# Turning attention probabilities with one stream transpose per head and moving the blocks by SBUF-to-SBUF transfers

## The chip, the cores and the metric

One core of a Trainium2 chip. The metric is the device time of one launch in microseconds (us), as a median of several runs. Each profile shows one execution on the chip.

## What is computed

Chunked attention with a few memory keys, then a two-layer network on its output:

```python
for c in range(S // 32):                       # S = 768, 4 batches, 8 heads of 64
    k_full = concat([mem_k, k[:, :, l_start:r_end]])   # 8 memory rows, 16 left, 32 own, 8 right
    scores = q_c @ k_full.T / 8;  a = softmax(scores)
    out_c = a @ v_full
x = out as (3072 tokens, 512)
h = x @ w_in                                   # 512 x 2048
g = s * relu(h) ** 2 + b
return g @ w_out                               # 2048 x 512
```

The weights arrive in 64 bits and are turned to floats on the chip. Every operand of a large product is split into a high and a low part (gH and gL, x high and x low, H and L of a weight), and a product is three matmuls.

## The kernel before

Tokens are worked on in eight pieces `ch` of 384 (two for each batch). For the first two batches (`ch` 0 to 3) the network runs directly: 64 steps `u`, each `hidden(u)` (line 811, 12 matmuls of 384 columns, L819) and `result(u)` (line 834, 9 matmuls of 512 columns, L843), with relu, square and affine on ScalarE (L827 to L830) and the low part gL on VectorE (L831) in between. For the last two batches the weights are combined (`mix`, line 908, L915 to L935), stored to a scratch in DRAM, fetched again (`fetch`, L945), and 16 units (`unit`, L978; `second`, L1028 and L1054) use fewer products.

`weight` (line 767) prepares one half weight: a transfer to one of three `words` tiles (L776), then VectorE (L800, L801, L803, L806) and ScalarE (L790, L796). `words` tiles are shared: weights use them, and a mix takes one for its sums (`m`) and one for each of its two stages.

`attend(ch, d)` (line 621) handles four heads of one piece, 16 visits in all. A visit has 96 matmuls for the scores (L656), two softmaxes `n` = 0, 1 over tiles of 128 x 6 x 64 (`softmax`, L563 to L582; the division is on GpSimd, L582), and later 48 matmuls with the values (L670). The probabilities must be turned before: `ch` 0 and 1 by TensorE (`turn`, line 592), the twelve visits of `ch` 2 to 7 by `flip` (line 609), 16 stream transposes of 32 x 96 (L613) for each softmax, each of which reads three 32 x 32 blocks and writes them to their place in the block-diagonal tile `aT`. What lies off the diagonal was set to zero once (L519).

The order of all work on each engine and of the transfers on SyncE's queue is fixed ahead of the run by a planner (`Plan.lay`, line 227): every operation has a priority (`prio`, mostly the step `u` at which it is due) and an expected duration (`HOLD`), and among those that are ready the lowest priority goes first. In the kernel each engine then works through its list in that order and waits where an operand is late. The planner expects a transfer to have landed 3400 ns (`FAR`) after its bytes were sent, and counts 440 ns on SyncE for an issue. GpSimd and VectorE operations marked `lock` are never planned at the same time. Constants such as `MIX`, `FLIPS`, `PROD`, `CHAIN`, `SECONDS` and `VISITS` are priorities. The score tiles of visit k and the values of visit k - 1 are issued one behind the other on TensorE.

Of the kernel before, what the change touches and what calls it, by code (L numbers as in the profile page):

```python
# [25 lines left out]
P = 128  # L26
QB = 128
# [56 lines left out]
AHEAD = 0.88  # L84
FLIPS = [5.12, 6.59, 6.68, 6.21, 6.01, 5.03, 6.84, 2.85, 10.89, 4.12, 6.97, 6.28]
PROD = [-1.21, 1.4, 1.6, 1.68, 2.1, 3.33, 3.43]
CHAIN = {'11': 2.04, '22': 0.52, '12': 3.22, '21': 4.37}
SECONDS = [2.94, 3.55, 8.0, 3.91]
XSUM = [-0.96, -0.62, 1.09, -0.07]
XSPLIT = [-6.05, -2.28, -0.26, -2.49, 0.78, 0.92, -0.32]  # L90
RBANKS = 2
# [15 lines left out]


PARTS = [0, 4, 10, NF]
# [6 lines left out]
UNIT = 3.75  # L116
VISITS = [41.16, 48.0, 50.14, 54.14, 58.95, 69.41, 72.68, 81.06, 85.03]
TURNED = set()

# [6 lines left out]
for _u, (_, _f) in enumerate(STEPS):  # L126
# [6 lines left out]
            relu=390, square=390, affine=565, high=388, xhigh=388, xhigh0=480, xhigh1=300, wscale=560, whigh=525, copy=270, exp6=480, exp3=340, keep=390, keepv=470, store=480,  # L133
            low=540, rec=90, edge=20, max6=490, max3=280, sub6=500, sub3=300, sum6=560, sum3=310, flip=270, xlow=470, xlow0=640, xlow1=400, wlow=350, wjoin=620, wsign=610, wdiff=610, out=600,
            small=235, part=290, wide=1040, tiny=200, norm6=1000, norm3=650, mul6=470, mul3=270, issue=440,
# [240 lines left out]
def body(ctx: ExitStack, tc: tile.TileContext, qkv, w1, w2, out):  # L376
# [67 lines left out]
    raws = ring("raw", 2, [P, QK], F32)  # L444
    ts_ = ring("t", 4, [QB, 2 * GB, CELL], F32)
    vs_ = ring("v", 2, [P, VW], F32)
    wide_ = [const.tile([P, 2 * GB * QB], F32, name=f"aT{i}") for i in range(2)]
    diags = Ring([x.rearrange("k (m c q) -> k m c q", m=GB, c=NQC) for x in wide_])
    stats = Ring(stat_tiles)
# [67 lines left out]
    op("POOL", "copy", -100, lambda: make_identity(nc, ident), (), (c_id[0],))  # L517
    for i, x in enumerate(wide_):
        op("POOL", "wrest", -99, lambda x=x: nc.gpsimd.memset(x, 0.0), (), (c_diag[i],))  # L519
    c_early, c_w = [fixed() for _ in range(NEARLY)], {x[1:]: fixed() for x in ORDER}  # L520
# [30 lines left out]

    def softmax(a, late, ch, S, t, st, rows, s_rows, fresh, unit=None):

# [3 lines left out]
        sv = lambda: S.tile[:, :2 * GB * CELL].rearrange("q (m k) -> q m k", k=CELL)[:, s_rows, :]  # L557
        tv = lambda: t.tile[:, rows, :]
        top, den, rden = (lambda k=k: st.tile[k][:, rows] for k in range(3))
        wide = lambda x: x().unsqueeze(2).to_broadcast([QB, n8, CELL])  # L560
        key = (rows.start, rows.stop)
        lo, hi, c, b = (0, LEFT, 0, 0) if ch % HALVES == 0 else (LEFT + CHUNK, LEFT + CHUNK + RIGHT, NQC - 1, GB - 1)
        op("DVE", "edge", a + 0.1, lambda: nc.vector.memset(sv()[c * CHUNK:(c + 1) * CHUNK, b::GB, lo:hi], NEG), (), fresh)  # L563
        op("DVE", "max" + size, a + 0.1, lambda: nc.vector.tensor_reduce(top(), sv(), axis=AX.X, op=ALU.max), fresh, (st["m", key],))
        if unit in SPLIT:
            small(a + 0.1, unit, lambda e: e.tensor_scalar(top(), top(), -SCALE, None, ALU.mult), (st["m", key],))
            for m in range(n8):
                op("ACT", "part", late + 0.2, lambda m=m: nc.scalar.activation(tv()[:, m, :], sv()[:, m, :], AF.Exp, bias=top()[:, m:m + 1], scale=SCALE,  # L568
                                                                               accum_out=den()[:, m:m + 1]),
                   (*fresh, st["m", key]), (t[key, m], st["d", key, m]))  # L570
            made_, sums = [t[key, m] for m in range(n8)], [st["d", key, m] for m in range(n8)]
        else:
            op("DVE", "sub" + size, a + 0.1, lambda: nc.vector.tensor_tensor(tv(), sv(), wide(top), ALU.subtract), (*fresh, st["m", key]), (t[key],))  # L573
            op("ACT", "exp" + size, late + 0.2, lambda: nc.scalar.activation(tv(), tv(), AF.Exp, scale=SCALE), (), (t[key],))
            op("DVE", "sum" + size, late + 0.25, lambda: nc.vector.tensor_reduce(den(), tv(), axis=AX.X, op=ALU.add), (t[key],), (st["d", key],))
            made_, sums = [t[key]], [st["d", key]]
# [15 lines left out]
    def turn(a, t, aT, need, unit):  # L592

        tp = Val(ps, "t")
        keep = lambda: tp.tile[:, :TOK].rearrange("k (m q) -> k m q", m=GB)
        tm = lambda m: t.tile.rearrange("q (m r) l -> q m (r l)", r=2)[:, m, :]
        for m in range(GB):
            op("PE", "turn", a + 0.3, lambda m=m: nc.tensor.transpose(keep()[:, m, :], tm(m), ident), (*need(m), c_id[0]), (tp[m],))
        for r in range(2):
            rows = slice(r * CELL, (r + 1) * CELL)  # L600
            to = lambda rows=rows, r=r: aT.tile[rows, :, :, r * CHUNK:(r + 1) * CHUNK]
            fro = lambda rows=rows: keep()[rows].rearrange("k m (c q) -> k m c q", c=NQC)
            got = [tp[m] for m in range(GB)]
            if (*unit, r) in KEEPV:
                op("DVE", "keepv", a + 0.3, lambda to=to, fro=fro: nc.vector.tensor_copy(to(), fro()), [*got, c_diag[0], c_diag[1]], (aT[r],))
            else:
                op("ACT", "keep", a + 0.3, lambda to=to, fro=fro: nc.scalar.activation(to(), fro(), AF.Copy), [*got, c_diag[0], c_diag[1]], (aT[r],))

    def flip(a, t, aT):

        def block(c, r, g):
            rows = slice(r * CELL + g * CHUNK, r * CELL + (g + 1) * CHUNK)
            nc.vector.transpose(aT.tile[rows, :, c, r * CHUNK:(r + 1) * CHUNK],  # L613
                                t.tile[c * CHUNK:(c + 1) * CHUNK, r::2, g * CHUNK:(g + 1) * CHUNK])

        for c in range(NQC):
            for r in range(2):
                for g in range(CELL // CHUNK):
                    op("DVE", "flip", a + 0.3, lambda c=c, r=r, g=g: block(c, r, g), [*t.parts.values(), c_diag[0], c_diag[1]], (aT[c, r, g],))

    def attend(ch, d):
# [41 lines left out]
        aT = []  # L663

        def value(m, V):
            for c in range(NQC):
                for n in range(2):
                    half, at = divmod(((m * NQC + c) * 2 + n) * D, VW)
                    to = V[m // 2].tile.rearrange("k (m r c q) -> k m r c q", r=2, c=NQC, q=CHUNK)[n * D:(n + 1) * D, m % 2, :, c, :]
                    nc.tensor.matmul(to, vals_[half].tile[:, at:at + D], aT[n].tile[:, m, c, :], start=True, stop=True)  # L670

# [20 lines left out]
        def reads(ms):  # L692
            halves = {((m * NQC + c) * 2 + 1) * D // VW for m in ms for c in range(NQC)}
            return [vals_[h][0] for h in sorted(halves)] + [z for y in aT for z in y.parts.values()]
# [12 lines left out]

        def soft(S):
            for n in range(2):
                t, y, st = Val(ts_), Val(diags), Val(stats)  # L710
                late = a + n * 0.5 if alone else a + BACK + n
                plan.group = (ch, d, n) if alone else None
                softmax(a + n * 0.5, late, ch, S[n], t, st, slice(0, 2 * GB), slice(0, 2 * GB), [S[n][p] for p in pairs], (ch, d, n))
                aT.append(y)
                if early or (ch, d) in TURNED:
                    turn(late, t, y, lambda m: t.parts.values(), (ch, d, n))
                else:
                    flip(a + FLIPS[max(0, 2 * (ch - NALONE) + d)] + n, t, y)

# [88 lines left out]

    g_vals, h_vals, a_vals, partial = {}, {}, {}, {}

    def hidden(u):
# [10 lines left out]
        for c in range(NC_T):  # L822
            op("PE", "hidden", H_AT(u), lambda c=c: products(c),
               (*(x[a, c // 2, r] for a in "HL" for r in range(2)), w["H"], w["L"]), (h[0],))
# [83 lines left out]
    def mix(j):  # L908
# [276 lines left out]
```

## Time and profile before

| | |
|---|---|
| median of 3 runs | 592.07 us (591.35 to 593.73) |
| the profiled execution | 592.51 us, of which the span is 590.7 us |
| TensorE busy | 578.8 us, 98% |
| VectorE busy | 441.7 us, 75% |
| ScalarE busy | 354.8 us, 60% |
| GpSimd busy | 41.7 us, 7% |
| granted clock of TensorE | 0.999 |

The span runs from the first to the last instruction; 1.8 us of the time lie around it. A busy TensorE is not one at its peak, since matmuls overlap and their ends are modelled: it is read together with the distance from one start to the next.

### The profile page before, as it was taken

Reading aid. Unit: us, or ns where it says so; the run is one execution under the profiler, and the core shown is the slowest. Engines: PE = TensorE matmul, PEld = TensorE weight load, DVE = VectorE, ACT = ScalarE, POOL = GpSimd, SP = SyncE. Lnnn points to the kernel's source line nnn. Section 1 sums busy time; section 2 is a strip of 40 time slices with the busy share of each in tenths; the row PEclk is TensorE's granted clock in tenths of the full one; section 3 lists DMA queues with packets and bytes.
Section 4 is the critical chain, followed back from the end, with each engine's and each line's share of the span. In section 5 each row is a group of like instructions: output and inputs, shape, how many; then the busy total and the mean of one; then the engine's idle time right before and its main releaser. Section 6 shows DMA issues by size and latency. Waiting matters only on the chain.

```text
span 590.7 us, 12521 instructions
## 1 busy us (share of the span) xinstructions
PE 578.8 (98%) x4961; PEld 512.2 (87%) x4961; DVE 441.7 (75%) x1100; ACT 354.8 (60%) x735; POOL 41.7 (7%) x50
## 2 busy tenths in 40 slices
PE   9989999999999999999999999999999999999997
PEld 4678988997889999898989989898899999999996
DVE  4988999787989887887888978697868543454443
ACT  6999876777665665555447555544547555444442
POOL 1000000000514010011012010101010000000000
PEclk9999999999999999999999999999999999999999
DMA  8996644548262544354256374643434452334102
GB/s 345 416 355 194 243 151 172 194 133 289 90 236 112 181 151 143 136 189 135 81 198 241 126 249 135 219 148 109 143 107 144 165 187 92 129 106 141 38 1 107
DMA packets 31178, 99.38 MB, mean 168 GB/s; under 512 B 3344, under 2 KB 5648, under 8 KB 31120
## 3 DMA queue, kind: packets, MB, share of 16 engines
q1 hardware_dynamic: 31120, 98.58, 48.0%
q8 instruction: 39, 0.64, 0.4%
q14 instruction: 19, 0.16, 0.1%
HBM read 77.60 MB, written 20.97 MB: 167 GB/s over the span
## 4 chain that ended last, share of the span: by engine, by line
PE 84%; DVE 7%; DMA 5%; ACT 2%; issue 1%; DVEq 0%; SPq 0%; ACTq 0%
PE ps L978 20%; PE ps L843 17%; PE ps L819 17%; PE ps L1028 11%; PE ps L1054 11%; PE ps L670 4%; DMA words<-w 3%; PE ps L656 3%; DVE aT L613 2%; DMA raw<-qkv 2%; DVE wv L801 1%; DVE wv L803 1%; DVE partial L863 1%; PE ps L512 1%; ACT t L568 1%
## 5 line engine op out<-in xcount | busy, mean ns | idle before, releaser
L613 DVE STREAM_TRANSPOSE aT<-t 32x96 f32<-32x96 f32 x384 | 103.4, 269 | 6.3
L978 PE MATMUL ps<-x,ww 128*128 128x384 f32 x384 | 73.2, 336 | 0.0
L819 PE MATMUL ps<-x,ww 128*128 128x384 f32 x384 | 71.8, 338 | 1.3 <-DVE t L573 0.5
L819 PE MATMUL ps<-x,home 128*128 128x384 f32 x384 | 72.5, 338 | 0.0
L819 PEld LDWEIGHTS ps<-x,ww 128*128 128x128 f32 x384 | 66.9, 188 | 4.2 <-ACT gH L830 0.9
L819 PEld LDWEIGHTS ps<-x,home 128*128 128x128 f32 x384 | 66.9, 188 | 2.2
L978 PEld LDWEIGHTS ps<-x,ww 128*128 128x128 f32 x384 | 67.3, 188 | 1.0
L827 ACT ACTIVATE ps<-ps 128x384 f32<-128x384 f32 x64 | 30.7, 480 | 61.1 <-PE ps L819 60.7
L985 ACT ACTIVATE wv<-ps 128x384 f32<-128x384 f32 x48 | 23.5, 490 | 63.3 <-PE ps L978 63.1
L843 PE MATMUL ps<-ww,gH 128*128 128x512 f32 x192 | 59.4, 390 | 0.0
L843 PE MATMUL ps<-w,gH 128*128 128x512 f32 x192 | 59.3, 390 | 0.0
L978 PE MATMUL ps<-home,ww 128*128 128x384 f32 x288 | 56.0, 336 | 0.0
L831 DVE TENSOR_TENSOR gL<-ps,gH 128x384 fp32r<-128x384 f32 x64 | 35.5, 554 | 23.1 <-ACT gH L830 20.8
L996 ACT ACTIVATE words<-words,b_sb,s_sb 128x384 f32<-128x384 f32 x64 | 45.1, 705 | 11.7 <-DVE words L995 10.7
L978 PEld LDWEIGHTS ps<-home,ww 128*128 128x128 f32 x288 | 50.7, 188 | 1.6
L994 DVE TENSOR_TENSOR words<-ps,wv 128x384 f32<-128x384 f32 x48 | 26.7, 557 | 29.9 <-PE ps L978 29.4
L582 POOL TENSOR_TENSOR t<-t,rden 128x384 f32<-128x384 f32 x24 | 21.5, 911 | 329.6 <-ACT x L688 71.8
L998 DVE TENSOR_TENSOR gL<-words,gH 128x384 fp32r<-128x384 f32 x47 | 26.2, 557 | 24.0 <-ACT gH L997 23.8
L829 ACT ACTIVATE ps<-ps,b_sb,s_sb 128x384 f32<-128x384 f32 x64 | 41.3, 645 | 2.0
L843 PEld LDWEIGHTS ps<-ww,gH 128*128 128x128 f32 x192 | 35.9, 188 | 7.2 <-DVE ww L806 0.4
L843 PEld LDWEIGHTS ps<-w,gH 128*128 128x128 f32 x192 | 36.1, 188 | 6.6
L1071 DVE TENSOR_TENSOR partial<-ps,partial 128x512 f32<-128x512 f32 x39 | 27.0, 691 | 17.8 <-PE ps L1054 17.6
(124 smaller groups left out, 1030.6 us busy)
## 6 DMA issues: line engine op xcount, KB each, us to landing
ww<-mixed SPq DMA_DIRECT2D x32, 512.0 KB, 3.4
raw<-qkv SPq DMA_DIRECT2D x28, 576.0 KB, 7.0
words<-w SPq DMA_DIRECT2D x24, 512.0 KB, 4.5
v<-qkv SPq DMA_DIRECT2D x28, 384.0 KB, 4.4
mixed<-words SPq DMA_DIRECT2D x16, 512.0 KB, 2.9
ww<-first SPq DMA_DIRECT2D x16, 512.0 KB, 3.7
out<-partial SPq DMA_DIRECT2D x23, 256.0 KB, 2.1
early<-w SPq DMA_DIRECT2D x8, 512.0 KB, 10.4
```

The source lines that it names most:

```text
L613: nc.vector.transpose(aT.tile[rows, :, c, r * CHUNK:(r + 1) * CHUNK], t.tile[c * CHUNK:(c + 1) * CHUNK, r::2, g * CHUNK:(g + 1) * CHUNK])
L819: nc.tensor.matmul(h.tile[:, :TOK], weight_tile(0, f)[:, wi, c * P:(c + 1) * P], xt(x, xi, c), start=(c == 0 and n == 0), stop=(c == NC_T ...
L827: op("ACT", "relu", u, lambda: nc.scalar.activation(hp(), hp(), AF.Relu), (), (h[0],))
L829: op("ACT", "affine", u, lambda: nc.scalar.activation(hp(), hp(), AF.Identity, scale=s_sb, bias=b_sb), (c_s[0], c_b[0]), (h[0],))
L831: op("DVE", "low", u, lambda: nc.vector.tensor_tensor(g.tile[1], hp(), g.tile[0].bitcast(F32), ALU.subtract), (h[0], g["H"]), (g["L"],))
L843: nc.tensor.matmul(acc.tile[:, lo:hi], g.tile[gi][:, t * P:(t + 1) * P], weight_tile(1, f)[:, wi, lo:hi], start=(first and n == 0), stop=( ...
L978: nc.tensor.matmul(bank.tile[:, :TOK], w(wi)[:, c * P:(c + 1) * P], operand(i, xi)[:, c * TOK:(c + 1) * TOK], start=start and c == 0 and n ...
L994: op("DVE", "hadd", at + prio, lambda: nc.vector.tensor_tensor(h.tile, bank.tile[:, :TOK], add.tile, ALU.add), (bank[0], add[0]), (h[0],))
L996: op("ACT", "haffine", at + prio, lambda: nc.scalar.activation(h.tile, h.tile, AF.Identity, scale=s_sb, bias=b_sb), (c_s[0], c_b[0]), (h[0],))
L1028: nc.tensor.matmul(to.tile, g.tile[gi][:, t * P:(t + 1) * P], weight_tile(1, f)[:, wi, :], start=start and n == 0, stop=stop and n == 2)
L1054: nc.tensor.matmul(r.tile[:, lo:hi], gd[1, order[n]].tile[gi][:, t * P:(t + 1) * P], weight_tile(1, 2 * j + order[n])[:, wi, lo:hi], start ...
L1071: op("DVE", "accum", at + SECONDS[3], lambda r=r, o=o: nc.vector.tensor_tensor(o.tile, r.tile, o.tile, ALU.add), (r[0],), (o[0],))
```

## The change

Only the twelve visits that used 16 transposes per softmax change in what they do. The probabilities of the two softmaxes of a visit now stand in one tile, with the order of columns changed from (cell of 64) to (half, cell, 32). One stream transpose of 128 x 384 per softmax turns all its 32 x 32 blocks in place. Eight transfers on SyncE's queue, SBUF to SBUF, of 48 KB each, then bring the blocks to the block-diagonal tile. That tile now holds both softmaxes, and a block pairs two chunks of 32 queries of one head instead of two heads of one chunk, so the order of the values in the input array changes too. The matmuls with the values are as many as before; they read two runs of 32 columns. Subtraction, sum and division of the softmax go through patterns with one dimension more.

Beside it, the sums of each `mix` get a dependency on step 24 (`RELEASE`), three of eight mixes (before: two) and two of the four `pre` sums (before: one) have GpSimd as their engine, and the priorities have other values. The expected duration of a transpose is set to 580 ns.

```diff
-MIX = [30.82, 32.64, 34.69, 47.24, 47.55, 47.83, 61.59, 43.54]
-MIXENG = ['DVE', 'POOL', 'DVE', 'POOL', 'DVE', 'DVE', 'DVE', 'DVE']
-XENG = ['DVE', 'POOL', 'DVE', 'DVE']
+MIX = [26.84, 28.58, 28.59, 35.13, 52.29, 42.51, 67.77, 47.04]
+MIXENG = ['POOL', 'POOL', 'DVE', 'POOL', 'DVE', 'DVE', 'DVE', 'DVE']
+XENG = ['DVE', 'DVE', 'POOL', 'POOL']
+RELEASE = 24
-FLIPS = [5.12, 6.59, 6.68, 6.21, 6.01, 5.03, 6.84, 2.85, 10.89, 4.12, 6.97, 6.28]
+FLIPS = [-1.9, 2.76, 8.24, 9.53, 3.67, 1.97, 9.18, 3.16, 11.4, 4.28, 12.19, 9.37]
...
-VISITS = [41.16, 48.0, 50.14, 54.14, 58.95, 69.41, 72.68, 81.06, 85.03]
+VISITS = [37.87, 44.33, 53.86, 55.97, 61.2, 70.58, 66.86, 83.36, 87.2]
...
+    both = ring("t", 2, [QB, 2, 2 * GB * CELL], F32)
...
+            op("DVE", "sub" + size, a + 0.1, lambda: nc.vector.tensor_tensor(tv(), like(sv()), wide(top), ALU.subtract), (*fresh, st["m", key]), (t[key],))
...
     def flip(a, t, aT):
-        def block(c, r, g):
-            rows = slice(r * CELL + g * CHUNK, r * CELL + (g + 1) * CHUNK)
-            nc.vector.transpose(aT.tile[rows, :, c, r * CHUNK:(r + 1) * CHUNK],
-                                t.tile[c * CHUNK:(c + 1) * CHUNK, r::2, g * CHUNK:(g + 1) * CHUNK])
...
+        for n in range(2):
+            op("DVE", "flip", a + n, lambda n=n: nc.vector.transpose(t.tile[:, n, :], t.tile[:, n, :]), (), [z for k, z in t.parts.items() if k[-1] == n])
+        made_ = list(t.parts.values())
+        w = GB * 2 * CHUNK
         for c in range(NQC):
+            for g in range(2):
+                row = (2 * (c // 2) + g) * CHUNK
+                op("SP", "issue", a + 1, lambda c=c, g=g, row=row: nc.sync.dma_start(
+                    aT.tile[row:row + CHUNK, :, c // 2, c % 2 * 2 * GB:(c % 2 + 1) * 2 * GB, :].rearrange("k n m q -> k n (m q)"),
+                    t.tile[c * CHUNK:(c + 1) * CHUNK, :, g * w:(g + 1) * w]), [*made_, c_diag[0], c_diag[1]], (aT[c, g],), size=CHUNK * 2 * w * 4)
...
+        def value2(m, V):
+            for m6 in (2 * m, 2 * m + 1):
+                for cp in range(2):
+                    for n in range(2):
+                        at = (((m6 % GB) * 2 + cp) * 2 + n) * D
+                        to = V[m // 2].tile.rearrange("k (m r c q) -> k m r c q", r=2, c=2, q=CHUNK)[n * D:(n + 1) * D, m6 % 4, :, cp, :]
+                        nc.tensor.matmul(to, vals_[m6 // GB].tile[:, at:at + D], aT[0].tile[:, n, :, cp * 2 * GB + m6, :], start=True, stop=True)
...
+            begun[u] = op("PE", "hidden", H_AT(u), lambda c=c: products(c),
...
+        for o in (wide_op(e, "mix2", at, lambda e: e.tensor_tensor(part(0, 2), two(f2, 0), two(f2, 1), ALU.add), (w2v["H"], w2v["L"]), (m[0], m[1])),
+                  wide_op(e, "mix2", at, lambda e: e.tensor_tensor(part(2, 4), two(f1, 0), two(f1, 1), ALU.add), (w1v["H"], w1v["L"]), (m[2], m[3]))):
+            o.deps.add(begun[RELEASE])
```

`PROD`, `CHAIN`, `SECONDS`, `XSUM`, `XSPLIT` and `AHEAD` (priorities inside the 16 units) have other values too.

## Rows read from the trace of the kernel before

**Rows 1.** The page: span, and busy time of each engine with its instructions.
```profile
span 590.7 us, 12521 instructions
PE 578.8 (98%) x4961; PEld 512.2 (87%) x4961; DVE 441.7 (75%) x1100; ACT 354.8 (60%) x735; POOL 41.7 (7%) x50
```

**Rows 2.** Windows: stretch, length, busy us of PE, PEld, DVE, ACT, POOL; clock, DMA.
```profile
60.00:100.00 40.00, 38.58 (x192) 34.03 (x191) 37.78 (x86) 32.49 (x63) 1.66 (x2) 1.00 0.53 182
135.00:168.00 33.00, 30.78 (x373) 26.59 (x373) 30.43 (x74) 20.68 (x40) 8.67 (x8) 1.00 0.49 173
168.00:587.00 419.00, 418.85 (x3379) 378.76 (x3364) 298.06 (x751) 223.35 (x422) 27.63 (x28) 1.00 0.42 143
```

**Rows 3.** TensorE in order of time, 86 to 100 us: start, busy; idle before, releaser.
```profile
86.90 0.45 PE L819 MATMUL ps<-x,ww 128*128 128x384 f32 x1 [0.20 <-ACT ww L796]
87.86 2.18 PE L819 MATMUL ps<-x,ww 128*128 128x384 f32 x11 [0.52 <-DVE ww L806]
...
99.30 0.50 PE L843 MATMUL ps<-w,gL 128*128 128x512 f32 x1 [0.66 <-DVE gL L831]
```

**Rows 4.** The same, 143 to 164 us.
```profile
143.25 2.33 PE L819 MATMUL ps<-x,ww 128*128 128x384 f32 x12 [0.54 <-DVE t L573]
...
154.38 0.50 PE L843 MATMUL ps<-ww,gL 128*128 128x512 f32 x1 [0.50 <-DVE gL L831]
...
163.62 0.50 PE L843 MATMUL ps<-ww,gL 128*128 128x512 f32 x1 [0.45 <-DVE gL L831]
```

**Rows 5.** The same, without idle time: one hidden block, one burst of values.
```profile
172.80 2.25 PE L819 MATMUL ps<-x,ww 128*128 128x384 f32 x12
...
201.83 1.62 PE L670 MATMUL ps<-aT,v 128*64 128x64 f32 x48
```

**Rows 6.** Groups by form: count, busy us, mean ns of one.
```profile
L613 DVE STREAM_TRANSPOSE aT<-t 32x96 f32<-32x96 f32 x384 | 103.4, 269 | 6.3
L819 PE MATMUL ps<-x,home 128*128 128x384 f32 x384 | 72.5, 338 | 0.0
L580 DVE TENSOR_TENSOR t<-t,rden 128x384 f32<-128x384 f32 x4 | 2.1, 549 | 0.0
```

**Rows 7.** One window of line L613 alone: busy us of VectorE, instructions.
```profile
60.00:100.00 40.00, 6.43 (x24) 1.00 0.53 182
```

**Rows 8.** VectorE in order of time: the first sum of the first mix.
```profile
54.04 0.69 DVE L922 TENSOR_TENSOR words<-home 128x512 f32<-128x512 f32 x1
```

**Rows 9.** VectorE in order of time, 141 to 163 us.
```profile
141.06 0.66 DVE L934 TENSOR_TENSOR words<-words,words 128x512 fp32r<-128x512 f32 x1
...
151.10 1.78 DVE L934 TENSOR_TENSOR words<-words,words 128x512 fp32r<-128x512 f32 x1
...
158.74 4.24 DVE L613 STREAM_TRANSPOSE aT<-t 32x96 f32<-32x96 f32 x15
163.00 0.56 DVE L831 TENSOR_TENSOR gL<-ps,gH 128x384 fp32r<-128x384 f32 x1
```

**Rows 10.** GpSimd in order of time: one sum of a mix.
```profile
150.59 1.74 POOL L923 TENSOR_TENSOR words<-home 128x512 f32<-128x512 f32 x1
```

**Rows 11.** Waits of SyncE's queue at L776: total us, times, longest us.
```profile
SPq L776 <- DVE wv L803: 51.5, 18, 5.9
```

**Rows 12.** Transfers by line: count, KB each, median us from issue to landing.
```profile
raw<-qkv SPq DMA_DIRECT2D x28, 576.0 KB, 7.0
...
v<-qkv SPq DMA_DIRECT2D x28, 384.0 KB, 4.4
...
out<-partial SPq DMA_DIRECT2D x2, 128.0 KB, 1.7
```

**Rows 13.** One visit in order of time: division, last transposes, values.
```profile
260.56 0.83 POOL L582 TENSOR_TENSOR t<-t,rden 128x384 f32<-128x384 f32 x1 [0.69 <-DVE rden L578]
...
268.49 2.00 DVE L613 STREAM_TRANSPOSE aT<-t 32x96 f32<-32x96 f32 x7
...
270.54 1.62 PE L670 MATMUL ps<-aT,v 128*64 128x64 f32 x48
```

More of the change, by code (lines that the diff above doesn't have):

```diff
@@ L116 @@
 UNIT = 3.75
-VISITS = [41.16, 48.0, 50.14, 54.14, 58.95, 69.41, 72.68, 81.06, 85.03]
-TURNED = set()
+VISITS = [37.87, 44.33, 53.86, 55.97, 61.2, 70.58, 66.86, 83.36, 87.2]
 def AT(k):
@@ L133 @@
             relu=390, square=390, affine=565, high=388, xhigh=388, xhigh0=480, xhigh1=300, wscale=560, whigh=525, copy=270, exp6=480, exp3=340, keep=390, keepv=470, store=480,
-            low=540, rec=90, edge=20, max6=490, max3=280, sub6=500, sub3=300, sum6=560, sum3=310, flip=270, xlow=470, xlow0=640, xlow1=400, wlow=350, wjoin=620, wsign=610, wdiff=610, out=600,
+            low=540, rec=90, edge=20, max6=490, max3=280, sub6=500, sub3=300, sum6=560, sum3=310, flip=580, xlow=470, xlow0=640, xlow1=400, wlow=350, wjoin=620, wsign=610, wdiff=610, out=600,
             small=235, part=290, wide=1040, tiny=200, norm6=1000, norm3=650, mul6=470, mul3=270, issue=440,
@@ L444, in body @@
     raws = ring("raw", 2, [P, QK], F32)
-    ts_ = ring("t", 4, [QB, 2 * GB, CELL], F32)
+    both = ring("t", 2, [QB, 2, 2 * GB * CELL], F32)
+    ts_ = Ring([x[:, n, :].rearrange("q (m k) -> q m k", k=CELL) for x in both.tiles for n in range(2)])
     vs_ = ring("v", 2, [P, VW], F32)
-    wide_ = [const.tile([P, 2 * GB * QB], F32, name=f"aT{i}") for i in range(2)]
-    diags = Ring([x.rearrange("k (m c q) -> k m c q", m=GB, c=NQC) for x in wide_])
+    wide_ = const.tile([P, 2, 2, GB * NQC, CHUNK], F32, name="aT")
+    diags = Ring([wide_[:, n] for n in range(2)])
+    diag = Ring([wide_])
     stats = Ring(stat_tiles)
@@ L517, in body @@
     op("POOL", "copy", -100, lambda: make_identity(nc, ident), (), (c_id[0],))
-    for i, x in enumerate(wide_):
-        op("POOL", "wrest", -99, lambda x=x: nc.gpsimd.memset(x, 0.0), (), (c_diag[i],))
+    for i in range(2):
+        op("POOL", "wrest", -99, lambda i=i: nc.gpsimd.memset(wide_[:, i], 0.0), (), (c_diag[i],))
     c_early, c_w = [fixed() for _ in range(NEARLY)], {x[1:]: fixed() for x in ORDER}
@@ L550, in xt, with softmax @@
         return x.tile[:, lo:lo + TOK]
-    def softmax(a, late, ch, S, t, st, rows, s_rows, fresh, unit=None):
+    def softmax(a, late, ch, S, t, st, rows, s_rows, fresh, unit=None, halved=None):
         n8 = len(range(*rows.indices(2 * GB)))
@@ L558, in softmax @@
         tv = lambda: t.tile[:, rows, :]
+        if halved is not None:
+            tv = lambda: t.tile[:, halved, :].rearrange("q (g m k) -> q m g k", g=2, m=2 * GB)
         top, den, rden = (lambda k=k: st.tile[k][:, rows] for k in range(3))
-        wide = lambda x: x().unsqueeze(2).to_broadcast([QB, n8, CELL])
-        key = (rows.start, rows.stop)
+        if halved is None:
+            wide = lambda x: x().unsqueeze(2).to_broadcast([QB, n8, CELL])
+            like = lambda x: x
+        else:
+            wide = lambda x: x().unsqueeze(2).unsqueeze(3).to_broadcast([QB, n8, 2, CHUNK])
+            like = lambda x: x.rearrange("q m (g k) -> q m g k", g=2)
+        key = (rows.start, rows.stop, halved)
         lo, hi, c, b = (0, LEFT, 0, 0) if ch % HALVES == 0 else (LEFT + CHUNK, LEFT + CHUNK + RIGHT, NQC - 1, GB - 1)
@@ L572, in softmax @@
         else:
-            op("DVE", "sub" + size, a + 0.1, lambda: nc.vector.tensor_tensor(tv(), sv(), wide(top), ALU.subtract), (*fresh, st["m", key]), (t[key],))
+            op("DVE", "sub" + size, a + 0.1, lambda: nc.vector.tensor_tensor(tv(), like(sv()), wide(top), ALU.subtract), (*fresh, st["m", key]), (t[key],))
             op("ACT", "exp" + size, late + 0.2, lambda: nc.scalar.activation(tv(), tv(), AF.Exp, scale=SCALE), (), (t[key],))
-            op("DVE", "sum" + size, late + 0.25, lambda: nc.vector.tensor_reduce(den(), tv(), axis=AX.X, op=ALU.add), (t[key],), (st["d", key],))
+            op("DVE", "sum" + size, late + 0.25, lambda: nc.vector.tensor_reduce(den(), tv(), axis=AX.X if halved is None else AX.XY, op=ALU.add), (t[key],), (st["d", key],))
             made_, sums = [t[key]], [st["d", key]]
@@ L600, in turn @@
             rows = slice(r * CELL, (r + 1) * CELL)
-            to = lambda rows=rows, r=r: aT.tile[rows, :, :, r * CHUNK:(r + 1) * CHUNK]
+            to = lambda rows=rows, r=r: aT.tile[rows, r].rearrange("k (m c) q -> k m c q", m=GB)
             fro = lambda rows=rows: keep()[rows].rearrange("k m (c q) -> k m c q", c=NQC)
@@ L663, in attend @@
         aT = []
+        def value2(m, V):
[5 more added lines that the diff above has]
+                        nc.tensor.matmul(to, vals_[m6 // GB].tile[:, at:at + D], aT[0].tile[:, n, :, cp * 2 * GB + m6, :], start=True, stop=True)
         def value(m, V):
+            if not early:
+                value2(m, V)
+                return
             for c in range(NQC):
@@ L669, in value @@
                     to = V[m // 2].tile.rearrange("k (m r c q) -> k m r c q", r=2, c=NQC, q=CHUNK)[n * D:(n + 1) * D, m % 2, :, c, :]
-                    nc.tensor.matmul(to, vals_[half].tile[:, at:at + D], aT[n].tile[:, m, c, :], start=True, stop=True)
+                    nc.tensor.matmul(to, vals_[half].tile[:, at:at + D], aT[n].tile[:, :, m * NQC + c, :], start=True, stop=True)
         def store(V):
@@ L692, in reads @@
         def reads(ms):
-            halves = {((m * NQC + c) * 2 + 1) * D // VW for m in ms for c in range(NQC)}
+            halves = {((m * NQC + c) * 2 + 1) * D // VW for m in ms for c in range(NQC)} if early else {m6 // GB for m in ms for m6 in (2 * m, 2 * m + 1)}
             return [vals_[h][0] for h in sorted(halves)] + [z for y in aT for z in y.parts.values()]
@@ L708, in soft @@
         def soft(S):
+            t, y = (None, None) if early else (Val(both), Val(diag))
             for n in range(2):
-                t, y, st = Val(ts_), Val(diags), Val(stats)
+                st = Val(stats)
                 late = a + n * 0.5 if alone else a + BACK + n
                 plan.group = (ch, d, n) if alone else None
-                softmax(a + n * 0.5, late, ch, S[n], t, st, slice(0, 2 * GB), slice(0, 2 * GB), [S[n][p] for p in pairs], (ch, d, n))
-                aT.append(y)
-                if early or (ch, d) in TURNED:
+                part, rows = [S[n][p] for p in pairs], slice(0, 2 * GB)
+                if early:
+                    t, y = Val(ts_), Val(diags)
+                    softmax(a + n * 0.5, late, ch, S[n], t, st, rows, rows, part, (ch, d, n))
+                    aT.append(y)
                     turn(late, t, y, lambda m: t.parts.values(), (ch, d, n))
                 else:
-                    flip(a + FLIPS[max(0, 2 * (ch - NALONE) + d)] + n, t, y)
+                    softmax(a + n * 0.5, late, ch, S[n], t, st, rows, rows, part, (ch, d, n), n)
+            if not early:
+                aT.append(y)
+                flip(a + FLIPS[2 * (ch - NALONE) + d], t, y)
         if ch == 0:
@@ L1133, in body @@
             later(o, before_x[i] if i < 7 else on(words) if i == 7 else plains(3, 4, 5))
+    for n in range(2):
+        hold(both, n, on(ts_))
+    hold(diag, 0, on(diags))
     for n in range(7):
@@ L1166 @@
     v2 = windows(v, mem_v).reshape(B, 2, 2, 2, HALVES, GB, NQC, CELL, D).transpose(0, 4, 1, 2, 5, 6, 3, 7, 8)
-    v2 = v2.reshape(B, HALVES, 2, GB, 2, NQC, 2, CELL, D).transpose(0, 1, 2, 4, 7, 3, 5, 6, 8).reshape(B, HALVES, 2, P, 2, VW)
-    v2 = v2.transpose(0, 1, 2, 4, 3, 5).reshape(B, HALVES, H // 2, P, VW)
+    first = v2[:1].reshape(1, HALVES, 2, GB, 2, NQC, 2, CELL, D).transpose(0, 1, 2, 4, 7, 3, 5, 6, 8).reshape(1, HALVES, 2, P, 2, VW)
+    first = first.transpose(0, 1, 2, 4, 3, 5).reshape(1, HALVES, H // 2, P, VW)
+    rest = v2[1:].reshape(B - 1, HALVES, 2, 2, GB, 2, 2, 2, CELL, D).transpose(0, 1, 2, 3, 5, 8, 4, 6, 7, 9).reshape(B - 1, HALVES, H // 2, P, VW)
+    v2 = np.concatenate([first, rest])
     sb = np.broadcast_to(np.stack([moe_s.reshape(()), moe_b.reshape(())]), q2.shape[:-1] + (2,))
```

20 lines of the change are left out of this document (7 added, 13 removed).

## Prediction

> **What bounds the kernel now.** I read the page first. TensorE is busy for 98% of the span, VectorE for 75%, and GpSimd hardly at all [rows 1]. So the question is not how much VectorE work goes, but where TensorE waits for it. The windows answer that: from 168 us to 587 us TensorE is busy 418.85 of 419.00 us, although VectorE works 298 us there [rows 2]. The reader is to see that nothing in these 419 us can get shorter by freeing VectorE; the matmuls themselves are the bound. The gaps lie earlier: 1.42 us idle from 60 to 100 us and 2.22 us from 135 to 168 us, both with VectorE over 90% busy [rows 2]. Before 60 us the change touches only the start of one mix: the first visits keep their way.
>
> TensorE in order of time shows six waits in these two stretches. Three stand at 86.90, 87.86 and 99.30 us (a weight's high part, a weight's low part, a gL) [rows 3], three at 143.25, 154.38 and 163.62 us (the subtraction of a softmax, then two gL) [rows 4].
>
> What one wait costs is more than its idle figure. Twelve matmuls take 2.25 us [rows 5] and a single one 0.338 us [rows 6], so one starts every (2.25 - 0.338)/11 = 0.174 us, and the modelled end lies 0.164 us behind the time at which the next could have started. The first matmul after a wait also takes about 0.11 us more (0.45 us at 86.90 us [rows 3] against 0.338). So each wait costs its idle time plus 0.27 us: (0.20 + 0.52 + 0.66) + 3 x 0.27 = 2.2 us in the first stretch, (0.54 + 0.50 + 0.45) + 3 x 0.27 = 2.3 us in the second. Together 4.5 us are all that this change can bring back, as far as the trace shows.
>
> **The transposes.** Removed are 384 of 269 ns, 103.4 us of VectorE [rows 6]. Added are 24 of 128 x 384. No row shows one: it takes at least what 32 x 96 takes, 0.269 us, and at most four times that, 1.08 us, if time goes with columns. I take 0.55 us, since another VectorE operation of 128 x 384 takes 0.549 [rows 6]. That is 24 x 0.55 = 13 us, and VectorE loses 90 us (77 to 97 by the bounds). 24 of the old ones lie in the first stretch, 6.43 us [rows 7], and the 32 of the second visit, 32 x 0.269 = 8.6 us, in the second. The other 328 lie beside a TensorE that does not wait; removing them is worth nothing.
>
> **The first stretch.** The first mix starts its sums at 54.04 us [rows 8], in the middle of the preparation of weights: three operations of 512 columns at 0.69 us and three of half that, some 3.1 us. It then keeps one of the three `words` tiles until its low part is made, the operation at 141.06 us [rows 9]. SyncE's queue waited 18 times, 51.5 us in all, for VectorE to free a tile for the next weight [rows 11]. With the release at step 24 (about 138 us, counted back by steps from the start of piece 2) this mix leaves the stretch, and weights have three tiles. VectorE loses 3.1 + 6.4 us and gains two transposes, 1.1 us: 8.4 us of relief against waits of 2.2 us. I count them as recovered: -2.2 us (bounds -2.2 and 0, if ScalarE or the loads are as late).
>
> **The second stretch.** The wait at 143.25 us is for the subtraction, in front of which stood the low part of that early mix at 141.06 us, 0.66 us [rows 9]; it is no longer there: -0.8 us. The gL before 163.62 us started at 163.00 us, right behind fifteen transposes in a row, 4.24 us [rows 9]; these are gone: -0.7 us. The gL before 154.38 us came late behind a low part of 1.78 us instead of 0.66 [rows 9], at a time when GpSimd ran a sum of a mix, itself 1.74 us [rows 10]. GpSimd's first mix now starts at about 140 us and can meet VectorE here again: 0 (bounds -0.8 and +0.8, one more such wait).
>
> A rule bears on that row. The Trainium skill (SBUF — State Buffer, "Who interferes with whom") says that a VectorE instruction with two SBUF inputs and a GpSimd instruction that reads SBUF exclude each other, and the later one waits for all of the other. The stretched pair of rows agrees. By the rule, two mixes by GpSimd from step 24 on would speak against this change; what that would do is a rival below, priced from rows.
>
> **The moved mixes.** All later mixes ran behind step 24 anyway; they stay within the 160 us before the units start, where VectorE has lost six visits of transposes, 6 x 32 x 0.269 = 52 us, and takes on one mix. Its cover is large: 0. GpSimd's extra sums (one mix, one `pre` for each batch) lie on an engine that is 7% busy: 0. The stores of the mixes wait on the queue for sums that end no later against their use: 0.
>
> **The transfers.** 12 x 8 = 96 issues on SyncE come in. Each waits for both transposes of its visit; behind it on the queue stand loads of weights and values and, later, fetches. What they replace is visible in one visit: the division ends at 260.56 + 0.83 = 261.39 us, the last transpose at 270.49 us, and the values start at 270.54 us [rows 13]. So the old hand-over took 9.1 us, and nothing stood between it and TensorE. The new one takes 2 x 0.55 for the transposes, 8 x 0.44 = 3.5 us of issues (the kernel's own allowance) and one landing. No row shows an SBUF-to-SBUF transfer. The nearest are 1.7 us for 128 KB out and 4.4 us for 384 KB in (as many bytes as the eight have), and the far end is 7.0 us for 576 KB in [rows 12]. I take 3 us, between the first two, as each is small but eight follow one another: 1.1 + 3.5 + 3 = 7.6 us, less than 9.1. The plan allows 3.4 us for the landing, so TensorE meets its values in time: 0 (bounds 0 and, with 7.0 us at eleven visits behind the first, 11 x 3.6 = +40 us, which is the third case below).
>
> The Trainium skill (DMA: Bandwidth & Descriptors, "Anatomy of one DMA") gives a fixed cost of about 2 us for a transfer, whatever its size. As an estimate from it, eight one behind the other would be 16 us, more than the old hand-over; side by side they would hide all but one. No row here decides between the two.
>
> **The other edits.** The matmuls with the values are 48 for each visit as before, 1.62 us for a burst [rows 5]. They now read two runs of 32 columns; they wrote their result in two runs before. No row shows the read. I take 0 (bounds: 0, since two runs are not read faster than one, and a doubled burst, 12 x 1.6 = +19 us, which I leave out of the range). Softmax operations with a dimension more do as many elements: 0, on VectorE with its new room. The new priorities inside the units change which result ends last: 0, within half a VectorE operation of 384 columns, 0.3 us either way.
>
> **The sum.** -2.2 - 0.8 - 0.7 = -3.7 us. The profiled execution took 592.51 us, its span 590.7 us. 592.51 - 3.7 = 588.8 us; the median lies 0.44 us under that execution, so 588.4 us. Half a per cent, 3 us, is about what a measurement of this kernel can tell from no change: the border lies at 589.1 us.
>
> **The rivals.**
> *Relief without effect.* The waits come back at other places: two mixes by GpSimd from step 24 on stretch VectorE operations among the last weights and gL, three or so times 0.8 us, and the queue brings the weights no earlier. For it speaks the stretched operation; against it, that the planner keeps marked operations apart and that the worst backlog, the transposes, is gone. Then -3.7 + 2.4 = -1.3 us, 590.8 us; within 589.1 and 595. That the transposes simply were not in TensorE's way is its extreme, 592.1 us.
> *The transfers come late.* The values stand in TensorE's fixed order where the plan expects them. From a landing of 3.4 us on, plus what SyncE is faster than 0.44 us an issue, each further microsecond is paid at up to eleven visits. At 4.4 us, the load of as many bytes, it is +11 us: 592.1 - 3.7 + 11 = 599.4 us, slower. Against it speaks 1.7 us for the smallest transfer, for it the eight on one queue among loads of 512 KB.
> *It does more than I see.* All 4.5 us come back and one more 0.8 us wait of another kind: 586.8 us. I count it with the forecast.
>
> **How the numbers follow.** Forecast, with all that ends under 589.1 us: 0.55. Relief without effect: 0.33. Late transfers: 0.12, of which a part (a landing just over the limit, less than 7 us lost in all) stays under 595 us; I move 0.01 to "same". The forecast's own bounds are 586.8 and 589.1 us; the range goes down by a further 0.8 us for a wait that I did not see, to 586.0, and up through most of the second case to 593.5 us, since that case alone holds a third. Over it stands about 0.13, under it 0.05.
>
> **What would show it.** Right: in 60 to 100 us and 135 to 168 us TensorE's idle time under 0.6 and 1.4 us (an issue stall of its own among them), no VectorE sum of a mix before 138 us, fewer waits at L776; a stream transpose near 0.55 us; VectorE near 352 us in all; TensorE still gapless behind 168 us. Wrong: waits for a transfer into `aT` in front of the values (the third case); L934 or L806 stretched and gL late at 140 to 165 us (the second); bursts of values longer than 1.62 us.

## The result and the profile after

The changed kernel takes 587.35 us as a median (586.88 to 587.61); beside it the kernel before took 592.37 us. The ratio is 0.9913, with an interval of 0.9891 to 0.9934: 0.87% faster. The profiled execution took 586.88 us.

The page after, its first two lines (answering to [rows 1]), the new transfers from its list of transfers (count, KB each, median us from the start of an issue to landing), and the waits of SyncE's queue at the load of the weights (answering to [rows 11]):

```profile
span 585.1 us, 12429 instructions
PE 575.4 (98%) x4956; PEld 512.3 (88%) x4961; DVE 347.5 (59%) x732; ACT 354.8 (61%) x735; POOL 50.3 (9%) x58
...
aT<-t SPq DMA_DIRECT2D x96, 48.0 KB, 2.0
...
SPq L802 <- DVE wv L829: 36.8, 16, 5.5
```

VectorE lost 94 us, the span 5.6 us. The windows of after (columns as in [rows 2]) say where:

```profile
60.00:100.00 40.00, 40.00 (x205) 36.51 (x204) 36.35 (x72) 34.38 (x67) 1.66 (x2) 1.00 0.74 259
100.00:135.00 35.00, 34.50 (x304) 30.94 (x303) 29.00 (x58) 26.15 (x51) 5.42 (x5) 1.00 0.58 195
135.00:168.00 33.00, 33.00 (x299) 29.93 (x298) 17.01 (x33) 20.62 (x42) 11.56 (x12) 1.00 0.42 143
168.00:582.00 414.00, 413.47 (x3295) 373.77 (x3293) 218.24 (x436) 220.69 (x416) 28.03 (x28) 1.00 0.44 150
```

TensorE's idle time from 60 to 100 us went from 1.42 to 0, that from 135 to 168 us from 2.22 to 0. In the first of these stretches VectorE still works 36.35 of 40 us, hardly less than before (37.78): weights that came later now come in it (L829 runs 13 times there, its counterpart L803 ran 10 times before). Behind 168 us VectorE does 80 us less, and TensorE, which had no gap there, gained nothing; the 0.53 us that it lacks in the last window lie behind its last matmul, which ends at 581.47 us.

All six waits of [rows 3, 4] are gone. One new wait stands between them, here with the rows around it (TensorE in order of time), and below it the turning of one visit (GpSimd, VectorE, SyncE's queue, TensorE; answering to [rows 13]) and one burst of values (to [rows 5]):

```profile
98.74 2.25 PE L845 MATMUL ps<-x,home 128*128 128x384 f32 x12
101.48 0.50 PE L869 MATMUL ps<-w,gL 128*128 128x512 f32 x1 [0.50 <-DVE gL L857]
...
241.58 1.62 POOL L590 TENSOR_TENSOR t<-t,rden 128x384 f32<-128x384 f32 x2 [15.32 <-ACT ps L854]
...
243.16 1.03 DVE L620 STREAM_TRANSPOSE t<-t 128x384 f32<-128x384 f32 x2
...
244.21 5.08 SPq L626 DMA_DIRECT2D aT<-t  x8
...
271.02 1.62 PE L680 MATMUL ps<-aT,v 128*64 128x64 f32 x48
```

The reader is to see the whole hand-over: the division ends at 243.20 us, the two transposes at 244.19, the eight issues at 249.29. The last of these began some 0.6 us before that, and a landing is counted from the start of its issue: with the median of 2.0 us the last block has landed at about 250.7 us, some 7.5 us behind the division. The values of this visit came only at 271 us; in six of the twelve visits they follow 7.6 to 8.7 us behind the second transpose, which is 8.6 to 13.0 us behind the division.

### The profile page after: what moved, and what is told of

Its sections match the earlier page's. It is cut to its first block, busy times and chain, and to the rows that moved or that the text cites. A ratio compares the mean times of both kernels' runs of the same rounds, so it can differ in the third digit from the quotient of the medians.

```text
span 585.1 us, 12429 instructions
## 1 busy us (share of the span) xinstructions
PE 575.4 (98%) x4956; PEld 512.3 (88%) x4961; DVE 347.5 (59%) x732; ACT 354.8 (61%) x735; POOL 50.3 (9%) x58
## 4 chain that ended last, share of the span: by engine, by line
PE 92%; ACT 3%; DMA 2%; DVE 2%; issue 1%; SPq 0%; ACTq 0%
PE ps L845 21%; PE ps L869 21%; PE ps L1005 20%; PE ps L1081 11%; PE ps L1055 11%; PE ps L680 3%; PE ps L665 3%; DMA early<-qkv 1%; DMA words<-w 1%; ACT t L576 1%; PE ps L690 1%; ACT wv L816 0%; DVE wv L827 0%; ACT ps L855 0%; PE ps L606 0%
## 5 line engine op out<-in xcount | busy, mean ns | idle before, releaser
L1005 PE MATMUL ps<-x,ww 128*128 128x384 f32 x384 | 75.1, 336 | 0.0
L845 PE MATMUL ps<-x,ww 128*128 128x384 f32 x384 | 71.4, 337 | 0.0
L1024 ACT ACTIVATE gH<-words 128x384 fp32r<-128x384 f32 x48 | 25.1, 524 | 50.2 <-PE ps L1081 48.1
L590 POOL TENSOR_TENSOR t<-t,rden 128x384 f32<-128x384 f32 x24 | 20.1, 852 | 300.0 <-DVE rden L586 61.5
L869 PE MATMUL ps<-w,gL 128*128 128x512 f32 x96 | 38.2, 398 | 1.3 <-DVE gL L857 1.3
L869 PE MATMUL ps<-ww,gL 128*128 128x512 f32 x96 | 37.6, 392 | 0.0
```

The costliest lines, as they stand in the source:

```text
L845: nc.tensor.matmul(h.tile[:, :TOK], weight_tile(0, f)[:, wi, c * P:(c + 1) * P], xt(x, xi, c), start=(c == 0 and n == 0), stop=(c == NC_T ...
L869: nc.tensor.matmul(acc.tile[:, lo:hi], g.tile[gi][:, t * P:(t + 1) * P], weight_tile(1, f)[:, wi, lo:hi], start=(first and n == 0), stop=( ...
L1005: nc.tensor.matmul(bank.tile[:, :TOK], w(wi)[:, c * P:(c + 1) * P], operand(i, xi)[:, c * TOK:(c + 1) * TOK], start=start and c == 0 and n ...
L1024: op("ACT", "hhigh", at + prio, lambda: nc.scalar.activation(g.tile[0], h.tile, AF.Copy), (h[0],), (g["H"],))
```

## Experiments

Each kernel is one of the two with the edit shown; times are medians, ratios are against the kernel before on the same chip, with their intervals.

### Before, with the dependency on step 24 alone

```diff
-            op("PE", "hidden", H_AT(u), lambda c=c: products(c),
+            begun[u] = op("PE", "hidden", H_AT(u), lambda c=c: products(c),
...
+        for o in (...the first two sums of a mix...):
+            o.deps.add(begun[RELEASE])
```

> The kernel before with the dependency on step 24 alone (old transposes, old priorities). Theory (VectorE's load and the words tile in the stage of the weights both count): no sum of a mix before 138 us, the waits at 86 to 100 us mostly gone (-1.5 to -2.2 us) and the one at 143 us (-0.8 us), the ones at 154 and 163 us stay: 589.3 to 590.3 us. Rival A (the transposes are the cause): no difference, 592 us, with the waits at 86 to 100 us in place. Rival B (the new priorities are the cause): 592 us.

587.89 us, ratio 0.9935 (0.9920 to 0.9950). TensorE has no wait from 40 us on but one of 0.94 us for a gL at 122.6 us; the first sum of a mix on VectorE starts at 137.92 us. One window (columns as in [rows 2]), that wait, and VectorE in order of time:

```profile
60.00:100.00 40.00, 40.00 (x205) 36.42 (x204) 38.48 (x82) 35.62 (x69) 1.66 (x2) 1.00 0.70 246
...
122.60 0.50 PE L844 MATMUL ps<-ww,gL 128*128 128x512 f32 x1 [0.94 <-DVE gL L832]
...
129.80 0.69 DVE L807 TENSOR_TENSOR ww<-wv,ww 128x512 fp32r<-128x512 f32 x1
...
137.92 0.68 DVE L923 TENSOR_TENSOR words<-home 128x512 f32<-128x512 f32 x1
...
153.58 3.95 DVE L614 STREAM_TRANSPOSE aT<-t 32x96 f32<-32x96 f32 x14
157.56 0.56 DVE L832 TENSOR_TENSOR gL<-ps,gH 128x384 fp32r<-128x384 f32 x1
```

The theory holds in its place and is too small in its size: the waits at 154 and 163 us went as well, although all old transposes are there. VectorE is not relieved in the first stretch: it works 38.48 us there, more than before. What changed is what it works on: the low part of the last weight (L807) is done at 130.5 us, where it was done at 151.2 us before. Old transposes still stand right in front of a gL, fourteen in a row before the one at 157.56 us, and TensorE does not wait for it; the row of fifteen alone was thus not enough for the wait at 163 us.

### The new turning alone, with old priorities and no dependency

```diff
-            o.deps.add(begun[RELEASE])
```

(and the constants of the kernel before in the changed kernel)

> The changed kernel with the old priorities and without the dependency on step 24: the new turning of the probabilities alone. Theory: VectorE is freed of 5.3 us in 60 to 100 us, but the early mix stays and keeps a words tile, so about half of the waits there remain; the wait at 163 us goes, those at 143 and 154 us stay: 589.8 to 591 us. Rival A (the transposes are the cause): 587 to 588 us. Rival B (priorities): 592 us, or slower, as the plan was laid for other durations.

589.0 us, ratio 0.9955 (0.9939 to 0.9971). TensorE in order of time, its two waits from 40 us on:

```profile
86.97 2.17 PE L845 MATMUL ps<-x,ww 128*128 128x384 f32 x11 [0.51 <-DVE ww L832]
...
95.06 0.73 PE L869 MATMUL ps<-ww,gH 128*128 128x512 f32 x2 [0.51 <-DVE ww L832]
```

Both are for a weight, in the stretch where the early mix still holds its tile. The second stretch has none, where two had been expected to stay. The time is a little better than the theory's. Its ten runs lie from 587.5 to 591.28 us, and the trace is that of the fastest; what the slower ones wait for is not shown.

### Turning and dependency, with old priorities

(the constants of the kernel before in the changed kernel, which keeps its dependency)

> The changed kernel with the old priorities (turning and dependency on step 24, nothing else). Theory: all that the change gives is in these two, 587 to 588.5 us. Rival B (priorities): 590 us or more. TensorE without waits at 60 to 100 us by the theory.

586.66 us, ratio 0.9915 (0.9900 to 0.9930), the same as the whole change within the intervals. So the new priorities bring nothing that these two do not. The two parts are not a sum: 0.65% and 0.45% alone, 0.85% together. They remove the same waits. With the dependency in place the turning adds 0.20 points, and the two intervals (0.9900 to 0.9930, 0.9920 to 0.9950) overlap: that it adds anything there is not shown beyond doubt.

### Before, with new priorities and dependency: the old transposes under the new order

> The kernel before with the new priorities and the dependency on step 24, with the old 16 transposes for each softmax. Theory: like the dependency alone, 589 to 590.5 us; the wait behind rows of old transposes (163 us) stays. Rival A: 592 us. Rival B (priorities): 587 to 588 us.

600.61 us, ratio 1.0145 (1.0128 to 1.0162): slower, which neither theory nor rival had. TensorE in order of time around the two largest losses and one hidden block behind the first, then two windows (columns as in [rows 2]):

```profile
239.24 0.34 PE L671 MATMUL ps<-aT,v 128*64 128x64 f32 x4 [0.81 <-DVE aT L614]
240.39 0.48 PE L671 MATMUL ps<-aT,v 128*64 128x64 f32 x4 [0.81 <-DVE aT L614]
241.55 2.18 PE L671 MATMUL ps<-aT,v 128*64 128x64 f32 x34 [0.68 <-DVE aT L614]
...
245.21 3.27 PE L820 MATMUL ps<-x,ww 128*128 128x384 f32 x12
...
264.21 0.79 PE L844 MATMUL ps<-w,gL 128*128 128x512 f32 x1 [5.41 <-DVE gL L832]
264.80 1.05 PE L844 MATMUL ps<-w,gH 128*128 128x512 f32 x2
...
261.00:267.00 6.00, 2.79 (x7) 2.21 (x8) 3.47 (x12) 0.00 (x0) 0.00 (x0) 0.50 0.07 26
268.00:275.00 7.00, 7.00 (x38) 6.51 (x37) 0.56 (x1) 4.53 (x10) 0.00 (x0) 1.00 0.01 2
```

The new priorities let a visit's values follow its softmax early, which they can where two transposes take 1.0 us. With the old ones VectorE ran 32 in a row, from 232.40 us for 9.10 us, and TensorE's fixed order waited for them; gL, put behind the next such row, came 5.4 us late. Behind both losses TensorE also ran at its lower clock for a while, 0.50 in the first window. So the priorities are no gain of their own but belong to the turning.

### What the early mix cost: the tile or VectorE's time

The first edit limits weights to two `words` tiles over the whole run, the second from the sixth load on, about 54 us, when the early mix took its tile. Both stand in the kernel before with the dependency.

```diff
-    words.room = lambda r, kind: kind is None or r.live.get(kind, 0) < (1 if kind == "mix" else 2)
+    words.room = lambda r, kind: r.live.get(kind, 0) < (1 if kind == "mix" else 2)
```

```diff
+    words.room = lambda r, kind: r.live.get(kind, 0) < (1 if kind == "mix" else 3 if kind is None and r.next.get(None, 0) < 5 else 2)
```

> The kernel before with the dependency on step 24 (587.9 us without more), and weights limited to two of the three words tiles: the early mix is gone from VectorE, but the tile that it held is still missing. If the tile is what the early mix cost, the waits for weights at 86 to 100 us come back and the queue waits some 50 us at the weights' load again: 589.5 to 591 us. If its time on VectorE is what it cost, TensorE has no wait from 60 to 100 us: 587.5 to 588.5 us.

> The kernel before with the dependency on step 24 (587.9 us without more), weights limited to two words tiles from the sixth load on, that is from about 54 us, when the early mix took its tile in the kernel before. VectorE is free of that mix, the tile is gone at just the same time. If the tile is what the early mix cost: waits for weights again before 100 us and 589.5 to 591 us. If VectorE's time is: no wait before 100 us and 587.5 to 588.5 us.

591.06 us, ratio 0.9981 (0.9969 to 0.9993), with waits of 1.69 and 0.80 us for weights at 86 and 87 us; and 589.85 us, ratio 0.9961 (0.9944 to 0.9978). TensorE's waits in the second, and VectorE's low part of the last weight, in this kernel and below it in the kernel before:

```profile
86.84 1.48 PE L820 MATMUL ps<-x,ww 128*128 128x384 f32 x7 [0.33 <-DVE ww L807]
...
98.27 0.49 PE L844 MATMUL ps<-w,gL 128*128 128x512 f32 x1 [0.66 <-DVE gL L832]
...
147.91 0.50 PE L844 MATMUL ps<-ww,gL 128*128 128x512 f32 x1 [0.57 <-DVE gL L832]
...
145.34 0.68 DVE L807 TENSOR_TENSOR ww<-wv,ww 128x512 fp32r<-128x512 f32 x1
...
149.88 1.30 DVE L806 TENSOR_TENSOR ww<-wv,ww 128x512 fp32r<-128x512 f32 x1
```

With the tile gone at the time at which the mix took it, and VectorE free of the mix, 0.26 of the 0.65 points are lost again, and a wait for a weight at 86.84 us is back. The two intervals (0.9944 to 0.9978, 0.9920 to 0.9950) overlap, so the size of the tile's part is uncertain; that it has a part shows in the weights, the last of which is done at 146.0 us, against 130.5 us with three tiles and 151.2 us before. The rest of the gain would be VectorE's time and order, which no run tried apart. The queue's waits at the weights' load told the tile's part badly: 15.3 us in this kernel against 37.0 us in the one with three tiles, which is faster. It waits less there because it waits at transfers in front of them: 20.7 us at L917, where the kernel with three tiles waits 9.3.

### The first mix on GpSimd

```diff
-MIXENG = ['DVE', 'POOL', 'DVE', 'POOL', 'DVE', 'DVE', 'DVE', 'DVE']
+MIXENG = ['POOL', 'POOL', 'DVE', 'POOL', 'DVE', 'DVE', 'DVE', 'DVE']
```

> The kernel before with the sums of the first mix on GpSimd instead of VectorE, no dependency on step 24: the tile is held from about 54 us, VectorE is free of 3.1 us. If the tile counts: 591 to 592.5 us. If VectorE's time counts: 589 to 590 us. If GpSimd's sums stretch VectorE's operations on two SBUF operands among the weights: L801, L803 or L806 of over 1 us at 54 to 65 us, and 592 us or more.

597.17 us, ratio 1.0079 (1.0053 to 1.0105). GpSimd had nothing else to do, so the mix began at 21 us and took the tile 33 us earlier than before. GpSimd and VectorE in order of time, and a wait of TensorE:

```profile
21.33 1.67 POOL L923 TENSOR_TENSOR words<-home 128x512 f32<-128x512 f32 x1 [16.37 <-DVE home L806]
23.63 1.66 POOL L922 TENSOR_TENSOR words<-home 128x512 f32<-128x512 f32 x1 [0.63 <-DVE home L806]
26.97 1.27 POOL L924 TENSOR_TENSOR words<-words 128x512 f32<-128x512 f32 x1
...
24.08 1.84 DVE L800 TENSOR_SCALAR early<-early 128x512 int32<-128x512 int32 x2
...
27.16 1.10 DVE L566 TENSOR_SCALAR top<-top 128x6 f32<-128x6 f32 x1
...
29.38 0.50 PE L843 MATMUL ps<-w,gL 128*128 128x512 f32 x1 [2.04 <-DVE gL L831]
```

Two VectorE operations at L800 take 1.84 us here; the same two took 0.76 us before, and the one at L566 0.15. The expected stretching is there, at 24 to 32 us and not at the times that were named. Both end behind a sum of GpSimd: that from 23.63 us ends at 25.29, the pair at L800 at 25.92; that from 26.97 us ends at 28.24, L566 at 28.26. GpSimd's own sums grow from 1.29 to 1.67 us. The Trainium skill (SBUF — State Buffer, "Who interferes with whom") lets the later of two such instructions wait for the whole of the other, also for VectorE's `tensor_scalar` in its two-port modes. The rows agree. The further loss lies at 43 us (1.59 us for a probability), at 89 to 91 us (1.87 and 1.07 us for a weight) and at 149 us (2.00 us); behind the waits at 29, 89 to 91 and 149 us the granted clock was 0.50 for a while. So this run does not part the tile from VectorE's time: the sums came too early for that.

### The changed kernel without the dependency

> The changed kernel without the dependency on step 24: mixes may start early again, the first ones on GpSimd. Theory: what the dependency gave beside the new turning, about 2 us, is lost: 588.5 to 590 us, with waits for weights before 100 us. Rival (VectorE is so free that it makes no difference): 587.3 us.

591.71 us, ratio 0.9988 (0.9975 to 1.0002): nothing is left of the gain. The loss is twice what was expected, and most of it does not lie where it was expected. With `MIXENG` of the changed kernel the first mix runs on GpSimd, again from 21 us, and TensorE waits 2.04 us for a gL at 29.3 us (0.80 us with the dependency) and 1.60 us for a probability at 43.6 us, with a granted clock of 0.50 for a while behind each; for weights it waits 0.28 and 0.37 us at 98 and 152 us. The dependency is what makes GpSimd's mixes harmless: in the changed kernel they run from 131 us on, when few weights are left.

### The transfers cut in halves

```diff
-                op("SP", "issue", a + 1, lambda c=c, g=g, row=row: nc.sync.dma_start(
-                    aT.tile[row:row + CHUNK, :, c // 2, c % 2 * 2 * GB:(c % 2 + 1) * 2 * GB, :].rearrange("k n m q -> k n (m q)"),
-                    t.tile[c * CHUNK:(c + 1) * CHUNK, :, g * w:(g + 1) * w]), ...
+                op("SP", "issue", a + 1, lambda c=c, g=g, row=row: [nc.sync.dma_start(
+                    aT.tile[row:row + CHUNK, n, c // 2, c % 2 * 2 * GB:(c % 2 + 1) * 2 * GB, :].rearrange("k m q -> k (m q)"),
+                    t.tile[c * CHUNK:(c + 1) * CHUNK, n, g * w:(g + 1) * w]) for n in range(2)], ...
```

> The changed kernel with each of the eight transfers of a visit cut in two halves of 24 KB, one behind the other, of which the plan knows nothing (same bytes, 16 issues). One issue of 48 KB takes 0.59 us now. If an issue costs the same whatever its size, the last block comes 8 x 0.59 = 4.7 us later, and at the visits where values follow within 8 to 9 us of the division (six of twelve) TensorE waits 3 to 4 us each: 605 to 612 us, with waits for the transfer in front of the values. If an issue costs by the number of its rows, nothing moves: 587.4 us. If TensorE had other work to put in: no change either, but transfers late.

615.16 us, ratio 1.0386 (1.0361 to 1.0411). The transfers' rows, the issues of one visit, TensorE's waits at another (in order of time), and the sum of TensorE's waits for these transfers (us, times, longest us):

```profile
aT<-t SPq DMA_DIRECT2D x192, 24.0 KB, 1.8
...
216.58 10.85 SPq L626 DMA_DIRECT2D aT<-t  x16
...
246.49 0.30 PE L680 MATMUL ps<-aT,v 128*64 128x64 f32 x2 [0.49 <-DMA aT<-t]
247.08 0.30 PE L680 MATMUL ps<-aT,v 128*64 128x64 f32 x2 [0.28 <-DMA aT<-t]
249.04 0.30 PE L680 MATMUL ps<-aT,v 128*64 128x64 f32 x2 [1.66 <-DMA aT<-t]
249.62 1.77 PE L680 MATMUL ps<-aT,v 128*64 128x64 f32 x42 [0.28 <-DMA aT<-t]
...
PE ps L680 <- DMA aT<-t: 13.2, 16, 2.5
```

An issue costs the same with half the bytes: sixteen take 10.85 us where eight took 5.08. The visits whose values follow soon wait 1.4 to 2.7 us each, six of them as expected (their values follow within 9 us of the second transpose, not of the division), 13.2 us in all. Not expected was the other part: the queue, held by sixteen issues from 83 to 96 us, sent the loads of weights late (VectorE waited 3.33 us for one at 102 us), and TensorE waited 4.58 us for a gL at 106 us. Behind that wait, and behind two of the six visits, the granted clock was 0.50 for a while (from 104 to 110, 251 to 253.5 and 333 to 335.5 us), which adds to the loss. So these transfers cost nothing where they are in time, and are dear to TensorE and to everything queued behind them where they are not.

### The kernel before once more

> The kernel before once more, for a second trace. If the six waits belong to its order of work, they stand at the same places within 1 us with the same releasers. The 0.73 us for which TensorE waited for nothing that the profile shows, in the scores at 138 us, recurs if it belongs to the program, and is gone if it was of that execution.

592.13 us. The six waits stand within 1.1 us of their places with the same releasers, a seventh of 0.45 us for a weight at 150.85 us beside them; the scores at 136 us run through in 1.20 us. The 0.73 us without a releaser did not recur, so it was of that one execution.

A fourth `words` tile, which would have shown the tile's part from the other side, was not tried.

## Why the prediction was right, step by step

- *The bound.* Right: a TensorE without gaps from 168 us on stayed so, and 80 us less of VectorE work there gave nothing. The kernel with the old transposes and the dependency alone shows it too: it is within 0.3% of the full change.
- *What a wait costs.* The sum agrees; the 0.27 us beside the idle time were not measured apart. The list of six waits came to 4.5 us. The span went down by 5.6: those 4.5, the execution's own stall at 138 us with its start-up (0.9), less the new wait at 101.48 us (0.50 + 0.27). About 1 us is left over, to which no row is put here.
- *The first stretch.* The size held (2.2 us, all recovered); the reason was wrong in part. I added 3.1 us of the mix to 6.4 us of transposes as one relief of VectorE. VectorE is hardly relieved there (37.78 us before, 36.35 after, 38.48 with the dependency alone, where TensorE has no gap either); it works on weights that are due. The runs show two things that overlap: the dependency alone clears the stretch with all transposes in place, the turning alone does not, and a part of the dependency's gain, 0.26 of 0.65 points with overlapping intervals, is the `words` tile.
- *The second stretch.* -0.8 and -0.7 us came as forecast, but not for the reasons that I had given each: the dependency alone, with all transposes, clears this stretch, and so does the turning alone, with the early mix. That the sum held is to this extent luck. For the gL at 154 us I had taken 0 of 0.8, and it came back too. This is the largest single term by which the forecast was too high. GpSimd's sums do run here now, from 146 to 152 us, but none of the low parts of a mix in this stretch is stretched: each takes 0.69 us, where one took 1.78.
- *The transposes.* 0.55 us taken, 0.568 measured; 352 us of VectorE forecast, 347.5 measured.
- *The transfers.* 7.6 us forecast for the hand-over, some 7.5 measured, and this from two errors that cancel: the eight issues take 5.1 us (3.5 taken), and the last block lands 1.4 us behind them (3 taken), as a landing of 2.0 us counts from the start of its issue. The Trainium skill (DMA: Bandwidth & Descriptors, "Anatomy of one DMA") gives about 2 us as fixed for a transfer, in a fit for transfers that GpSimd issues. The trace agrees with 2.0 us for these on SyncE's queue, and they lie side by side, one started every 0.64 us. The point at which lateness is paid was right, the price somewhat high: some 5.8 us more of issues cost waits of 1.4 to 2.7 us at six visits and not the whole at eleven, since values of the other visits follow late. What I missed is the loads behind them on the queue.
- *Relief without effect.* Not what happened, but its mechanism is real: 597.17 and 591.71 us where GpSimd's mixes are let into the stage of the weights, in the first of them with stretched operations of VectorE.
- *The other edits.* A burst of values takes 1.62 us as before. The new priorities are worth nothing with the new turning, as forecast; that they do harm with the old one (600.61 us, against 587.89 us with the dependency alone) I had not seen.

## What to carry to other kernels

Where the bounding engine has no gaps, count the gaps one by one where it has them and forecast their sum, not the work removed: 94 us less of VectorE came with 5 us, and the dependency alone, which removes nothing, gave four of the five. A gap that a sum explains is not yet explained by each of its terms: two edits can remove the same wait. A buffer that an early side task holds can cost beside its instructions, so ask of every task that starts as soon as it can what it keeps from the one that is due. An order tuned to fast hand-overs must not be put over slow ones, and a hand-over by transfers is costed by its issues on the queue, one by one, and by what waits behind them.

## Hardware that I had not expected

- An SBUF-to-SBUF transfer of these holds SyncE's queue for 0.59 us at 48 KB and at 24 KB (medians), while loads of 512 KB from DRAM took 0.33 us to issue.
- Behind long waits TensorE ran at the lower of its two clock levels. In the kernel with new priorities and old transposes the granted clock is 0.50 (1.2 GHz) from 261 to 267 us, in and behind the wait of 5.41 us, and 1.00 (2.4 GHz) from 268 us on: two matmuls of 512 columns started 0.42 us apart at 264.8 us instead of 0.23. It is 0.50 from 241 to 247 us too, behind the three waits of 0.7 to 0.8 us at 238 to 242 us: the twelve matmuls of 384 columns at 245.21 us took 3.27 us, where twelve take 2.25.
